# The first pair's first half taken one head at a time, with its row maxima brought to the scores by one copy

## The chip, the cores and the metric

One core of a Trainium2 chip runs the whole program. The metric is device time in microseconds (us) of one execution, as the median of several runs. PE is TensorE (PEld its weight loads), DVE VectorE, ACT ScalarE, POOL GpSimd, SP the engine whose queue issues most transfers.

## The reference, cut to what matters

Attention with a mask from clusters (a query sees the keys whose nearest of 16 centroids is its own), then two dense layers.

```python
# q, k, v: (2, 8, 768, 64); x: 1536 tokens of 512; w_in: 512 x 2048, w_out: 2048 x 512
mask = q_assign[:, :, :, None] == k_assign[:, :, None, :]
scores = scale * np.matmul(q, k.transpose(0, 1, 3, 2))
scores = np.where(mask, scores, -1000000000.0)
scores = scores - np.max(scores, axis=-1, keepdims=True)
attn = np.exp(scores)
attn = attn / (np.sum(attn, axis=-1, keepdims=True) + 1e-09)
x = np.matmul(attn, v)            # then, with heads joined:
h = np.maximum(x @ w_in, 0.0);  x = h * h @ w_out
h = x @ w_in2;  g = h * np.cos(h);  out = g @ w_out2
```

## The kernel before

**Tiling.** The 16 heads go in 8 pairs. In a pair's tiles one head (j = 0) lies in partitions 0 to 63 and the other (j = 1) in 64 to 127, so a matmul for one head contracts over 64 partitions, one half of the PE array's rows. The 768 tokens are two halves of 384, or six tiles of 128. Each of q and k is split into a rounded part (`hq`, `hk`) and a rest (`lq`, `lk`); they lie in tiles that the profile calls `set`. `ext` holds `xq` and `xk`, one-hot rows of the clusters, which make the mask.

**A half of a pair**, in steps, each a small function:

- `s_max` (matmul L579): four matmuls fill one *unit*, a piece of PSUM of two banks, [128 queries, 2, 384]: for each head the product of one query tile with one half of the keys, and the mask's product on top. There are three units, shared by nearly all steps here. `s_largest` (L589) takes the largest over the keys on DVE and so gives the unit back. Six of these (three query tiles, two halves of keys) give the maxima of both heads over 384 queries.
- `max_parts` (L598, DVE) joins the two halves of the keys, `max_cast` (L604, ACT) spreads each maximum over 32 columns, `max_rows` (L613, PE) turns them into rows by three matmuls with the identity, `max_keep` (L620, ACT) copies those out of PSUM, `stage_max` (L627, two transfers) puts them into the outer rows of `lq`.
- `scores` (L648): eight matmuls, four products for each of the two heads, give a unit [128 keys, 2 heads, 384 queries]; the fourth product reads `lq` with the maxima and so subtracts them. Of the first three units of all (`APART`) the fourth product stands apart, in `scores_end`. `exponent` (L662, ACT) reads the unit and gives it back, `add_up` (L674, POOL) adds the exponentials, `pv` (L682, PE) multiplies by v into `o_ps`, `sums` (L699), `move_out` (L737) and others finish the half.

In all matmuls of `s_max` and `scores` the two heads alternate: j = 0, j = 1, j = 0, and so on.

**The masks of the following pairs** are made in between, from `sims` (L466) over `by_token` (L484), `at_max` (L507), `compare` (L514) and `one_hot` (L520) to `keep_one_hot` (L527). `keep_warm` (L774) are matmuls without a use, which stand on PE where it would wait.

**Order.** `PLACES` gives every step a number, by hand; all steps are sorted by it and written out once, and each engine runs its own instructions in that order. The dense layers (L885, L939) come after, also in a fixed order.

Of the kernel before, what the change touches and what calls it, by code (L numbers as in the profile page):

```python
# [9 lines left out]
F32 = mybir.dt.float32  # L10
# [6 lines left out]
AX = mybir.AxisListType.X  # L17
# [12 lines left out]
N_WARM = 23  # L30
# [8 lines left out]
        3, 2, 24, 58, 60, 79, 176, 179, 301, 332, 418, 529, 597, 613, 733, 701,  # L39
    ),  # L40
    "low_part": (
        9, 42, 70, 59, 69, 126, 295, 217, 351, 404, 472, 531, 641, 630, 787, 715,
    ),
    "load_raw": (
        25, 240, 0, 43, 283, 140, 178, 428, 239, 287, 480, 350, 417, 634, 481, 580, 828, 583, 644, 898,
    ),
    "sims": (
        6, 28, 77, 227, 338, 504, 581, 696,
    ),
    "keep_sims": (  # L50
        12, 35, 78, 228, 341, 505, 582, 697,
    ),
    "by_token": (
        21, 47, 96, 252, 376, 523, 653, 724,
    ),
    "largest": (
        22, 48, 117, 259, 407, 524, 654, 726,
    ),
    "spread": (
        23, 75, 118, 272, 425, 546, 661, 734,  # L60
    ),
    "at_max": (
        31, 80, 132, 275, 433, 547, 663, 755,
    ),
    "compare": (
        33, 83, 151, 289, 437, 548, 675, 779,
    ),
    "stage_own": (
        87, 196, 251, 397, 352, 611, 616, 819,
    ),  # L70
    "stage": (
        10, 5, 111, 88, 222, 226, 331, 303, 443, 416, 555, 571, 649, 673, 809, 795,
    ),
    "one_hot_k": (
        40,
    ),
    "one_hot_q": (
        44,
    ),
    "keep_k": (  # L80
        41,
    ),
    "keep_q": (
        45,
    ),
    "max_parts": (
        82, 128, 173, 223, 305, 356, 406, 464, 545, 578, 664, 707, 781, 823, 887, 941,
    ),
    "max_cast": (
        89, 131, 174, 235, 313, 364, 427, 466, 554, 579, 665, 728, 782, 824, 888, 942,  # L90
    ),
    "max_rows": (
        90, 136, 194, 253, 321, 377, 435, 491, 564, 608, 666, 729, 783, 836, 903, 951,
    ),
    "max_keep": (
        91, 139, 195, 255, 322, 378, 436, 492, 566, 609, 667, 730, 786, 839, 904, 959,
    ),
    "stage_max": (
        98, 141, 210, 256, 347, 379, 444, 500, 584, 612, 668, 744, 802, 862, 913, 960,
    ),  # L100
    "one_hot": (
        93, 191, 318, 442, 562, 680, 780,
    ),
    "keep_one_hot": (
        95, 192, 319, 449, 563, 686, 791,
    ),
    "stage_oh": (
        120, 224, 345, 450, 599, 689, 817,
    ),
    "squares": (  # L110
        7, 26,
    ),
    "norms": (
        8, 27,
    ),
    "inverses": (
        11, 34,
    ),
    "keep_warm": (
        13, 14, 15, 16, 17, 18, 19, 20, 29, 30, 36, 37, 38, 39, 46, 49, 50, 51, 52, 53, 64, 65, 66,  # L120
    ),
    "constants_own": (
        1, 32, 4,
    ),
    "constants": (
        81, 94,
    ),
    "move_out": (
        202, 231, 320, 380, 446, 509, 569, 656, 693, 745, 838, 865, 899, 948, 981,
    ),  # L130
    "sums": (
        242, 360, 493, 606, 714, 834, 949, 996,
    ),
    "move_sums": (
        243, 361, 494, 610, 717, 841, 956, 997,
    ),
    "deal_sums": (
        244, 363, 501, 615, 718, 842, 958, 1001,
    ),
    "invert": (  # L140
        276, 385, 508, 643, 727, 847, 968, 1011,
    ),
    "store_inverse": (
        277, 392, 510, 658, 756, 870, 969,
    ),
    "load_inverse": (
        286, 398, 514, 672, 765, 900, 974,
    ),
    "divide": (
        326, 339, 429, 457, 561, 592, 725, 721, 804, 769, 930, 931, 1005, 1000,  # L150
    ),
    "combine_high": (
        327, 342, 465, 458, 575, 607, 731, 732, 844, 784, 950, 935, 1006, 1002,
    ),
    "combine_low": (
        329, 368, 537, 476, 589, 671, 797, 762, 849, 902, 980, 986, 1010, 1007,
    ),
    "s_max": (
# [5 lines left out]
    ),  # L164
    "s_largest": (
# [5 lines left out]
    ),  # L171
    "scores": (
# [15 lines left out]
    ),  # L188
    "add_up": (
# [5 lines left out]
    ),  # L195
# [22 lines left out]
def tile_kernel(ctx: ExitStack, tc: tile.TileContext, lead, behind, q, k, v, directions, centroids, w1i, w1o, w2i, w2o, out):  # L218
    nc = tc.nc
# [373 lines left out]
    def max_parts(n, hf):
# [3 lines left out]
        m1 = ap.tile([P, 2 * HT], F32, tag="m1", name=f"m1{n}{hf}", bufs=2)  # L597
# [25 lines left out]
    def stage_max(n, hf, e=nc.sync):  # L623
# [622 lines left out]
```

## Time and profile before

| | us |
|---|---|
| median of 3 runs | 747.66 (747.25 to 747.78) |
| the profiled execution | 747.83 |
| its span in the trace | 746.1 |

The profiled execution is 0.17 above the median, and 1.7 of it lies outside the span. On the page and in the views, busy time is the union of an engine's records; the records of matmuls overlap, so a stretch in which PE is busy throughout can still hold small waits. PE is busy in 737.4 of 746.1 us, DVE in 577.4, ACT in 352.9, POOL in 248.3.

### The profile page before, as it was taken

Reading aid. Unit: us, or ns where it says so; the run is one execution under the profiler, and the core shown is the slowest. Engines: PE = TensorE matmul, PEld = TensorE weight load, DVE = VectorE, ACT = ScalarE, POOL = GpSimd, SP = SyncE. Lnnn points to the kernel's source line nnn. Section 1 sums busy time; section 2 is a strip of 40 time slices with the busy share of each in tenths; the row PEclk is TensorE's granted clock in tenths of the full one; section 3 lists DMA queues with packets and bytes.
Section 4 is the critical chain, followed back from the end, with each engine's and each line's share of the span. In section 5 each row is a group of like instructions: output and inputs, shape, how many; then the busy total and the mean of one; then the engine's idle time right before and its main releaser. Section 6 shows DMA issues by size and latency. Waiting matters only on the chain.

```text
span 746.1 us, 11041 instructions
## 1 busy us (share of the span) xinstructions
PE 737.4 (99%) x4143; PEld 573.2 (77%) x4143; DVE 577.4 (77%) x913; ACT 352.9 (47%) x595; POOL 248.3 (33%) x249
## 2 busy tenths in 40 slices
PE   8999999999999999999999999999999999999997
PEld 5766766666667888888888888888887888888886
DVE  6897988896689999697883149699998766676664
ACT  5655656564555464635445344544334333343332
POOL 8899998999996200000000000022221000000000
PEclk9999999999999999999999999999999999999999
DMA  6525433314534610474000037420001000010001
GB/s 209 165 88 160 124 119 103 113 45 142 196 116 161 225 57 1 144 245 147 29 0 1 1 95 238 147 84 1 0 2 55 2 1 1 0 57 1 0 1 56
DMA packets 40589, 62.18 MB, mean 83 GB/s; under 512 B 6228, under 2 KB 28760, under 8 KB 40536
## 3 DMA queue, kind: packets, MB, share of 16 engines
q1 hardware_dynamic: 40200, 60.65, 25.4%
q10 hardware_dynamic: 336, 0.84, 0.3%
q8 instruction: 32, 0.52, 0.3%
q14 instruction: 21, 0.17, 0.1%
HBM read 48.46 MB, written 5.29 MB: 72 GB/s over the span
## 4 chain that ended last, share of the span: by engine, by line
PE 85%; DVE 12%; issue 1%; DMA 1%; ACT 1%; SPq 0%; DVEq 0%
PE bank L939 30%; PE bank L885 15%; PE o_ps L885 14%; PE unit L648 9%; PE o_ps L682 9%; PE unit L579 5%; DVE ews L908 3%; DVE ews L907 1%; DVE m L589 1%; DVE ews L919 1%; DVE top L324 1%; PE o_ps L466 1%; DVE aux L322 1%; PE o_ps L699 1%; DVE ews L910 1%
## 5 line engine op out<-in xcount | busy, mean ns | idle before, releaser
L674 POOL TENSOR_TENSOR acc<-acc,p 128x384 f32<-128x384 f32 x128 | 142.1, 1143 | 1.0 <-ACT p L662 0.8
L939 PE MATMUL bank<-w,ewr 128*128 128x512 f32 x576 | 138.2, 389 | 0.6 <-DVE w L317 0.6
L939 PE MATMUL bank<-ewr,w 128*128 128x512 f32 x576 | 138.5, 389 | 0.0
L924 POOL TENSOR_TENSOR ewr<-ews,ewr 128x512 fp32r<-128x512 f32 x22 | 29.5, 1340 | 299.6 <-ACT ewr L920 289.2
L885 PE MATMUL bank<-xh,w 128*128 128x512 f32 x392 | 128.7, 390 | 0.0
L939 PEld LDWEIGHTS bank<-w,ewr 128*128 128x128 f32 x576 | 108.0, 188 | 23.4 <-DVE w L317 1.0
L939 PEld LDWEIGHTS bank<-ewr,w 128*128 128x128 f32 x576 | 108.0, 188 | 22.7 <-ACT ews L901 0.3
L885 PE MATMUL o_ps<-xh,w 128*128 128x512 f32 x376 | 123.3, 389 | 0.0
L589 DVE TENSOR_REDUCE m<-unit 128x2 f32<-128x768 f32 x96 | 88.9, 950 | 25.7 <-PE unit L579 22.6
L662 ACT ACTIVATE p<-unit 128x768 f32<-128x768 f32 x96 | 73.4, 813 | 50.8 <-PE unit L648 44.7
L924 DVE TENSOR_TENSOR ewr<-ews,ewr 128x512 fp32r<-128x512 f32 x74 | 51.7, 698 | 51.6 <-ACT ewr L903 46.9
L885 PEld LDWEIGHTS bank<-xh,w 128*128 128x128 f32 x392 | 73.5, 188 | 16.5 <-issue 1.2
L911 ACT ACTIVATE ews<-ews,narrow_t 128x512 f32<-128x512 f32 x48 | 34.8, 725 | 100.5 <-DVE ews L910 100.5
L885 PEld LDWEIGHTS o_ps<-xh,w 128*128 128x128 f32 x376 | 70.5, 188 | 14.5
L885 PE MATMUL bank<-xl,w 128*128 128x512 f32 x196 | 76.3, 389 | 0.0
L885 PE MATMUL o_ps<-xl,w 128*128 128x512 f32 x188 | 73.1, 389 | 0.0
L682 PE MATMUL o_ps<-p,rawv 128*64 128x384 f32 x384 | 68.1, 493 | 0.0
L648 PE MATMUL unit<-set,set 64*128 64x384 f32 x512 | 67.1, 342 | 0.1
L905 DVE TENSOR_SCALAR ews<-ews 128x512 f32<-128x512 f32 x48 | 20.3, 422 | 43.4 <-ACT ews L915 43.1
L324 DVE SCALAR_TENSOR_TENSOR top<-wraw,top 128x512 uint32<-128x512 uint32 x64 | 51.1, 799 | 1.6
L648 PEld LDWEIGHTS unit<-set,set 64*128 64x128 f32 x512 | 45.3, 184 | 6.8 <-ACT p L662 2.6
L322 DVE SCALAR_TENSOR_TENSOR aux<-wraw,aux 128x512 f32<-128x512 uint32 x64 | 49.1, 767 | 1.6
(141 smaller groups left out, 1026.4 us busy)
## 6 DMA issues: line engine op xcount, KB each, us to landing
wraw<-in_moe_w_in_dram SPq DMA_DIRECT2D x32, 512.0 KB, 3.9
wraw<-in_moe_w_out_dram SPq DMA_DIRECT2D x32, 512.0 KB, 4.3
ext<-set SPq DMA_DIRECT2D x32, 96.0 KB, 2.9
rawv<-in_v_dram SPq DMA_DIRECT2D x8, 384.0 KB, 3.5
rb<-row SPq DMA_DIRECT2D x14, 192.0 KB, 3.5
fq<-in_q_dram SPq DMA_DIRECT2D x6, 384.0 KB, 4.1
fk<-in_k_dram SPq DMA_DIRECT2D x6, 384.0 KB, 3.7
held<-kept SPq DMA_DIRECT2D x8, 256.0 KB, 3.1
```

The lines of the kernel that those rows point to most:

```text
L322: cost(690, lambda: ve.scalar_tensor_tensor(restf, low, 2.0**-32, rest, ALU.mult, ALU.add)),
L324: cost(690, lambda: ve.scalar_tensor_tensor(top, high, 0xC0000000, top, ALU.bitwise_and, ALU.bitwise_or)),
L579: nc.tensor.matmul(u[:, j, :HALF], lhsT=a[r, qs], rhs=b[r, ks], start=(p == 0), stop=(p == 1))
L589: nc.vector.tensor_reduce(d["m"][:, i, :, kh], u[:, :, :HALF], AX, ALU.max)
L648: nc.tensor.matmul(u[:, j, :HALF], lhsT=a[r], rhs=b[r, qs], start=(p == 0), stop=(p == len(ops) - 1))
L662: nc.scalar.activation(t, u[:, :, :HALF], AF.Exp, scale=SCALE)
L674: nc.gpsimd.tensor_tensor(accs[hb][:, j], a[:, j], ptiles[u_][:, j], ALU.add)
L682: nc.tensor.matmul(o_ps[0][j * D : (j + 1) * D, :HALF], lhsT=raw[n, "v"][:, kt, j, :], rhs=t[:, j], start=(kt == 0), stop=(kt == NT - 1),)
L885: nc.tensor.matmul(ph, lhsT=w[:, a, :], rhs=x[blk][:, a, :], start=(a == i == 0), stop=(a == KD - 1 and i == 2))
L911: nc.scalar.activation(e2, e2, AF.Sin, bias=hpi)
L924: e.tensor_tensor(al, e2, ah.bitcast(F32), ALU.subtract)
L939: nc.tensor.matmul(y, lhsT=a, rhs=b, start=(idx in opens and i == 0), stop=(idx in closes and i == 2))
```

## The change

For the first half of the first pair alone (units 0 to 5), a unit holds one head: its two banks are the two halves of the keys in `s_max`, and two tiles of keys in `scores`. One reduction over both banks (`AXY`) then gives the final maximum of a head, into a small tile `by_head`; three units finish a head. `max_rows` for this half takes a column of `by_head`, repeated 128 times, as its weights, three matmuls for each head, so that every row of the result holds the maxima; `max_keep` copies the 32 rows that `lq` needs straight into it. `max_parts`, `max_cast` and `stage_max` fall away for this half. `add_up` and `pv` of this half take their operands by the new split. Three `keep_warm` go (`N_WARM` 23 to 20), and the numbers in `PLACES` are new up to about 400, above that nearly all are the old ones less 4.

```diff
-N_WARM = 23
+N_WARM = 20
...
     "s_max": (
-        61, 62, 54, 67, 71, 73, 86, 84, 97, 100, 103, 116, 163, 171, 154, 148, 125, 149, 200, 218, 197, 214,
+        58, 60, 66, 68, 50, 74, 82, 80, 86, 94, 100, 119, 156, 169, 146, 137, 126, 132, 195, 208, 207, 188,
...
     "scores": (
-        102, 119, 106, 123, 112, 146, 161, 165, 159, 167, 157, 175, 233, 215, 229, 260, 247, 249, 284, 292,
...
+        101, 96, 116, 107, 121, 138, 149, 159, 154, 163, 151, 165, 227, 222, 218, 257, 244, 241, 267, 277, 272,
...
+    by_head = prepp.tile([P, 64], F32R, name="by_head")[:, :NT].rearrange("p (j t) -> p j t", j=2)
+
     def s_max(u_):
         n, c = divmod(u_, SP)
         i, kh = divmod(c, 2)
         d = pd[n]
         u = unit()
-        qs, ks = slice(i * P, (i + 1) * P), slice(kh * HALF, (kh + 1) * HALF)
+        if u_ < NT:
+            kh, i = divmod(u_, HT)
         for p, (a, b) in enumerate(((d["hq"], d["hk"]), (xq[n % 2], xk[n % 2]))):
             for j in range(2):
-                r = slice(j * D, (j + 1) * D)
+                head, part = (kh, j) if u_ < NT else (j, kh)
+                r = slice(head * D, (head + 1) * D)
+                qs, ks = slice(i * P, (i + 1) * P), slice(part * HALF, (part + 1) * HALF)
                 nc.tensor.matmul(u[:, j, :HALF], lhsT=a[r, qs], rhs=b[r, ks], start=(p == 0), stop=(p == 1))
...
-        nc.vector.tensor_reduce(d["m"][:, i, :, kh], u[:, :, :HALF], AX, ALU.max)
+        if u_ < NT:
+            nc.vector.tensor_reduce(by_head[:, u_ // HT, u_ % HT : u_ % HT + 1], u[:, :, :HALF], AXY, ALU.max)
+        else:
+            nc.vector.tensor_reduce(d["m"][:, i, :, kh], u[:, :, :HALF], AX, ALU.max)
...
-    def max_rows(n, hf):
+    def max_rows(n, hf, j=None):
         d = pd[n]
         u = unit()
+        if j is not None:
+            for t in range(HT):
+                nc.tensor.matmul(
+                    u[:, 0, t * P : (t + 1) * P], lhsT=by_head[:, j, t : t + 1].to_broadcast([P, P]), rhs=identr,
+                    start=True, stop=True,
+                )
+            d["mru", j] = u
+            return
...
-    def max_keep(n, hf):
-        d = pd[n]
+    def max_keep(n, hf, j=None):
+        d = pd[n]
+        if j is not None:
+            u = d.pop(("mru", j))
+            nc.scalar.copy(d["lq"][OUTER[j], hf * HALF : (hf + 1) * HALF], u[OUTER[j], 0, :HALF])
+            give(u)
+            return
...
         for p in mine:
-            a, b = ops[p]
             for j in range(2):
-                r = slice(j * D, (j + 1) * D)
+                head, t = (j, kt) if u_ >= NT else (kt // HT, kt % HT * 2 + j)
+                ks = slice(t * P, (t + 1) * P)
+                ops = (
+                    (d["hk"][:, ks], d["hq"]), (d["lk"][:, ks], d["hq"]), (xk[i][:, ks], xq[i]),
+                    (block(sets[n % 3], t), d["lq"]),
+                )
+                a, b = ops[p]
+                r = slice(head * D, (head + 1) * D)
...
+        if hb == 0:
+            for i in (0, 1) if kt == 1 else (kt,):
+                j = i // HT
+                y, t = accs[hb][:, j], ptiles[i]
+                a, b = (t[:, 0], t[:, 1]) if i % HT == 0 else (y, t[:, 0])
+                nc.gpsimd.tensor_tensor(y, a, b, ALU.add)
+                if i % HT:
+                    nc.gpsimd.tensor_tensor(y, y, t[:, 1], ALU.add)
+            return
...
         for j in range(2):
+            i, c = (u_, j) if u_ >= NT else (kt // 2 + j * HT, kt % 2)
...
-                o_ps[0][j * D : (j + 1) * D, :HALF], lhsT=raw[n, "v"][:, kt, j, :], rhs=t[:, j],
+                o_ps[0][j * D : (j + 1) * D, :HALF], lhsT=raw[n, "v"][:, kt, j, :], rhs=ptiles[i][:, c],
```

The lines of the kernel move by 5 to 35; L579 becomes L584, L589 L596 (this half) and L598, L613 L622 (this half) and L630, L620 L637 (this half) and L642, L648 L674, L682 L717.

**On PE, from the seventh `s_max` to the first unit of `scores`.** `set0_0`, `set0_1` are the first pair's `hq`, `hk`; `set0_2`, `set0_3` its `lq`, `lk`; `x2` counts matmuls. Before:

```order
L579 MATMUL unit1_71<-set0_1_101,set0_0_100 128x384 x2
L579 MATMUL unit1_71<-ext0_1_113,ext0_0_112 128x384 x2
L579 MATMUL unit2_72<-set0_1_101,set0_0_100 128x384 x2
L579 MATMUL unit2_72<-ext0_1_113,ext0_0_112 128x384 x2
L613 MATMUL unit0_70<-identr_78,set0_3_103 64x128 x3
...
L484 MATMUL o_ps1_66<-ident_73,sc2_333 128x128 x3
L579 MATMUL unit0_70<-set0_1_101,set0_0_100 128x384 x2
...
L579 MATMUL unit2_72<-set0_1_101,set0_0_100 128x384 x2
...
L648 MATMUL unit1_71<-set0_0_100,set0_1_101 128x384 x2
```

Now, from `sims` of the third pair on:

```order
L466 MATMUL o_ps1_66<-fk2_289,cb_120 32x384 x2
L622 MATMUL unit2_72<-identr_78,by_head_119 128x128 x3
L584 MATMUL unit0_70<-set0_1_101,set0_0_100 128x384 x2
...
L584 MATMUL unit2_72<-set0_1_101,set0_0_100 128x384 x2
...
L622 MATMUL unit1_71<-identr_78,by_head_119 128x128 x3
L584 MATMUL unit0_70<-set0_1_101,set0_0_100 128x384 x2
...
L484 MATMUL o_ps1_66<-ident_73,sc2_340 128x128 x3
...
L584 MATMUL unit1_71<-set0_1_101,set0_0_100 128x384 x2
L584 MATMUL unit1_71<-ext0_1_113,ext0_0_112 128x384 x2
L674 MATMUL unit0_70<-set0_0_100,set0_1_101 128x384 x2
```

Two groups of `max_rows` stand where one stood, one for each head, and the first `scores` still follow the tenth `s_max`. The rows name no partitions: in the first six `s_max` and `scores` both matmuls of an `x2` are now of one head.

**On ACT, around the first exponentials.** `mxb`, `sc` are of the masks of later pairs. Before:

```order
L440 CAST set2_1_109<-fk2_271 128x768
L604 CAST set0_3_103<-m100_341 128x192
L620 CAST mr00_362<-unit0_70 64x384
L627 DMA set0_2_102<-mr00_362 32x384
L662 ACTIVATE p0_403<-unit1_71 128x768
```

Now:

```order
L440 CAST set2_1_109<-fk2_289 128x768
L637 CAST set0_2_102<-unit2_72 32x384
L476 ACTIVATE sc2_340<-o_ps1_66,narrow_t_85 128x384
L637 CAST set0_2_102<-unit1_71 32x384
L688 ACTIVATE p1_384<-unit0_70 128x768
```

A cast, a copy and a transfer (with its twin on SP) became two copies; the first exponential is that of the second unit.

## Rows read from the trace of the kernel before

**Rows 1.** The page, parts 1 and 2: busy us, share, instructions; granted clock.

```profile
PE 737.4 (99%) x4143; PEld 573.2 (77%) x4143; DVE 577.4 (77%) x913; ACT 352.9 (47%) x595; POOL 248.3 (33%) x249
...
PEclk9999999999999999999999999999999999999999
```

**Rows 2.** Busy time by stretch: PE, PEld, DVE, ACT, POOL, clock, DMA.

```profile
13.20:25.00 11.80, 10.50 (x83) 6.39 (x85) 11.58 (x17) 5.00 (x9) 11.33 (x9) 1.00 0.49 145
25.00:60.00 35.00, 35.00 (x307) 23.87 (x309) 30.98 (x44) 20.17 (x33) 30.32 (x27) 1.00 0.44 132
60.00:230.00 170.00, 169.83 (x1413) 113.52 (x1410) 141.25 (x164) 100.46 (x173) 164.61 (x155) 1.00 0.43 133
```

**Rows 3.** The chain that ended last, 11 to 32 us: start, us, what.

```profile
13.94 5.29 DVE m L589 x6
...
19.25 0.17 DVE m L598
...
22.11 1.83 DVE m L589 x2
...
23.99 1.84 PE unit L648 x16
```

**Rows 4.** Timeline of ACT: start, us, engine, line, idle before.

```profile
19.71 0.35 ACT L604 CAST set<-m 128x192 fp32r<-128x192 f32 x1
20.55 0.47 ACT L620 CAST mr<-unit 64x384 fp32r<-64x384 f32 x1 [0.48 <-PE unit L613]
```

**Rows 5.** Timeline of PE, same columns, from 24.8 us: units one behind the other.

```profile
24.85 0.62 PE L648 MATMUL unit<-set,set 64*128 64x384 f32 x4
25.31 0.34 PE L648 MATMUL unit<-ext,ext 64*128 64x384 f32 x2
25.49 0.34 PE L648 MATMUL unit<-set,set 64*128 64x384 f32 x2
25.67 0.33 PE L579 MATMUL unit<-set,set 64*128 64x384 f32 x2
```

**Rows 6.** The weight loads (PEld) of the same stretch.

```profile
25.32 0.19 PEld L648 LDWEIGHTS unit<-set,set 64*128 64x128 f32 x2
```

**Rows 7.** A stretch of the dense layers, PE alone: matmuls of 512 columns.

```profile
300.00:350.00 50.00, 50.00 (x222) 1.00 0.55 179
```

**Rows 8.** Timeline of DVE from 13.2 us.

```profile
13.94 5.28 DVE L589 TENSOR_REDUCE m<-unit 128x2 f32<-128x768 f32 x6 [0.15 <-PE unit L579]
...
19.34 0.55 DVE L514 TENSOR_TENSOR free_xh<-free_xl,unit 128x384 bf16<-128x384 f32 x1
19.80 1.81 DVE L589 TENSOR_REDUCE m<-unit 128x2 f32<-128x768 f32 x2
21.53 0.67 DVE L527 TENSOR_SCALAR free_xl<-unit,oh_above,oh_scale 128x384 fp32r<-128x384 f32 x1
```

**Rows 9.** Timeline of PE at the first scores.

```profile
22.25 0.62 PE L648 MATMUL unit<-set,set 64*128 64x384 f32 x4
...
23.12 0.45 PE L579 MATMUL unit<-set,set 64*128 64x384 f32 x2
23.41 0.34 PE L579 MATMUL unit<-ext,ext 64*128 64x384 f32 x2
23.59 1.02 PE L648 MATMUL unit<-set,set 64*128 64x384 f32 x6
...
24.62 0.34 PE L648 MATMUL unit<-set 64*128 64x384 f32 x2
```

**Rows 10.** Timeline of PE around the end of the first half.

```profile
38.58 2.16 PE L682 MATMUL o_ps<-p,rawv 128*64 128x384 f32 x12
40.67 0.34 PE L520 MATMUL o_ps<-eq,first_of 128*128 128x384 bf16 x1
```

**Rows 11.** Timeline of PE from 13.2 us: `sims` and `at_max` among the maxima.

```profile
17.23 0.52 PE L466 MATMUL o_ps<-fq,cb 128*32 128x384 f32 x2
...
18.34 0.55 PE L507 MATMUL unit<-ident,free_xl 128*128 128x128 f32 x3
```

More of the change, by code (lines that the diff above doesn't have):

```diff
@@ L16 @@
 ALU = mybir.AluOpType
-AX = mybir.AxisListType.X
+AX, AXY = mybir.AxisListType.X, mybir.AxisListType.XY
 PSUM = bass.MemoryType.PSUM
@@ L46 @@
     ),
     "sims": (
-        6, 28, 77, 227, 338, 504, 581, 696,
+        7, 21, 75, 209, 319, 500, 577, 692,
     ),
     "keep_sims": (
-        12, 35, 78, 228, 341, 505, 582, 697,
+        9, 40, 78, 210, 332, 501, 578, 693,
     ),
     "by_token": (
-        21, 47, 96, 252, 376, 523, 653, 724,
+        18, 42, 91, 251, 372, 519, 649, 720,
     ),
     "largest": (
-        22, 48, 117, 259, 407, 524, 654, 726,
+        19, 51, 99, 254, 403, 520, 650, 722,
     ),
     "spread": (
-        23, 75, 118, 272, 425, 546, 661, 734,
+        22, 56, 105, 284, 421, 542, 657, 730,
@@ L61 @@
     ),
     "at_max": (
-        31, 80, 132, 275, 433, 547, 663, 755,
+        25, 64, 129, 286, 429, 543, 659, 751,
     ),
     "compare": (
-        33, 83, 151, 289, 437, 548, 675, 779,
+        28, 65, 157, 287, 433, 544, 671, 775,
     ),
     "stage_own": (
-        87, 196, 251, 397, 352, 611, 616, 819,
+        69, 153, 292, 393, 352, 607, 612, 815,
     ),
     "stage": (
-        10, 5, 111, 88, 222, 226, 331, 303, 443, 416, 555, 571, 649, 673, 809, 795,
+        27, 8, 113, 104, 221, 216, 347, 310, 439, 412, 551, 567, 645, 669, 805, 791,
@@ L73 @@
     ),
     "one_hot_k": (
-        40,
+        33,
     ),
     "one_hot_q": (
-        44,
-    ),
-    "keep_k": (
-        41,
-    ),
-    "keep_q": (
-        45,
+        36,
+    ),
+    "keep_k": (
+        43,
+    ),
+    "keep_q": (
+        44,
+    ),
+    "max_rows": (
+        76, 85, 131, 184, 255, 303, 373, 431, 487, 560, 604, 662, 725, 779, 832, 899, 947,
+    ),
+    "max_keep": (
+        77, 87, 135, 185, 256, 304, 374, 432, 488, 562, 605, 663, 726, 782, 835, 900, 955,
     ),
@@ L86 @@
     "max_parts": (
-        82, 128, 173, 223, 305, 356, 406, 464, 545, 578, 664, 707, 781, 823, 887, 941,
+        122, 171, 228, 276, 329, 402, 460, 541, 574, 660, 703, 777, 819, 883, 937,
     ),
     "max_cast": (
[L90 to L96, printed above, removed]
+        128, 172, 232, 300, 359, 423, 462, 550, 575, 661, 724, 778, 820, 884, 938,
@@ L97 @@
     ),
     "stage_max": (
-        98, 141, 210, 256, 347, 379, 444, 500, 584, 612, 668, 744, 802, 862, 913, 960,
+        136, 217, 264, 320, 375, 440, 496, 580, 608, 664, 740, 798, 858, 909, 956,
     ),
     "one_hot": (
-        93, 191, 318, 442, 562, 680, 780,
+        92, 183, 301, 438, 558, 676, 776,
     ),
     "keep_one_hot": (
-        95, 192, 319, 449, 563, 686, 791,
+        93, 187, 302, 445, 559, 682, 787,
     ),
     "stage_oh": (
-        120, 224, 345, 450, 599, 689, 817,
+        125, 220, 349, 446, 595, 685, 813,
@@ L109 @@
     ),
     "squares": (
-        7, 26,
+        3, 20,
     ),
     "norms": (
-        8, 27,
+        4, 37,
     ),
     "inverses": (
-        11, 34,
+        5, 39,
     ),
     "keep_warm": (
-        13, 14, 15, 16, 17, 18, 19, 20, 29, 30, 36, 37, 38, 39, 46, 49, 50, 51, 52, 53, 64, 65, 66,
+        10, 11, 12, 13, 14, 15, 16, 17, 23, 24, 29, 30, 31, 32, 41, 45, 46, 47, 48, 49,
     ),
     "constants_own": (
-        1, 32, 4,
+        0, 38, 2,
     ),
     "constants": (
-        81, 94,
+        63, 83,
@@ L127 @@
     ),
     "move_out": (
-        202, 231, 320, 380, 446, 509, 569, 656, 693, 745, 838, 865, 899, 948, 981,
+        186, 230, 307, 376, 442, 505, 565, 652, 689, 741, 834, 861, 895, 944, 977,
     ),
     "sums": (
-        242, 360, 493, 606, 714, 834, 949, 996,
+        237, 355, 489, 602, 710, 830, 945, 992,
     ),
     "move_sums": (
-        243, 361, 494, 610, 717, 841, 956, 997,
+        238, 356, 490, 606, 713, 837, 952, 993,
     ),
     "deal_sums": (
-        244, 363, 501, 615, 718, 842, 958, 1001,
+        252, 357, 497, 611, 714, 838, 954, 997,
@@ L139 @@
     ),
     "invert": (
-        276, 385, 508, 643, 727, 847, 968, 1011,
+        253, 381, 504, 639, 723, 843, 964, 1007,
     ),
     "store_inverse": (
-        277, 392, 510, 658, 756, 870, 969,
+        296, 388, 506, 654, 752, 866, 965,
     ),
     "load_inverse": (
-        286, 398, 514, 672, 765, 900, 974,
+        298, 394, 510, 668, 761, 896, 970,
     ),
     "divide": (
-        326, 339, 429, 457, 561, 592, 725, 721, 804, 769, 930, 931, 1005, 1000,
+        308, 317, 425, 453, 557, 588, 721, 717, 800, 765, 926, 927, 1001, 996,
@@ L209 @@
-        961, 970, 972, 993, 995, 998, 999,
+        34, 103, 110, 111, 115, 134, 148, 161, 162, 179, 180, 181, 214, 215, 243, 250, 271, 285, 295, 366, 378,
+        392, 401, 430, 466, 471, 509, 549, 592, 594, 627, 646, 688, 702, 712, 762, 882, 886, 925, 933, 939,
+        957, 966, 968, 989, 991, 994, 995,
     ),
     "begin_moe": (
-        858,
+        854,
     ),
@@ L587, in s_largest @@
         if "m" not in d:
-            d["m"] = ap.tile([P, NT, 2, 2], F32, tag="m", name=f"m{n}", bufs=2)
-        nc.vector.tensor_reduce(d["m"][:, i, :, kh], u[:, :, :HALF], AX, ALU.max)
+            m = ap.tile([P, R], F32, tag="m", name=f"m{n}", bufs=2)[:, : 4 * NT]
+            d["m"] = m.rearrange("p (t j h) -> p t j h", j=2, h=2)
+        if u_ < NT:
+            nc.vector.tensor_reduce(by_head[:, u_ // HT, u_ % HT : u_ % HT + 1], u[:, :, :HALF], AXY, ALU.max)
+        else:
+            nc.vector.tensor_reduce(d["m"][:, i, :, kh], u[:, :, :HALF], AX, ALU.max)
         give(u)
@@ L596, in max_parts @@
         mm = d["mm"] = sets[n % 3][3][:, S : S + HT * 2 * R].rearrange("p (t r) -> p t r", t=HT)
-        m1 = ap.tile([P, 2 * HT], F32, tag="m1", name=f"m1{n}{hf}", bufs=2)
+        m1 = ap.tile([P, R], F32, tag="m1", name=f"m1{n}{hf}", bufs=2)[:, : 2 * HT]
         nc.vector.tensor_reduce(m1.rearrange("p (t j) -> p t j", j=2), m, AX, ALU.max)
@@ L621, in max_keep, with stage_max @@
         give(u)
-    def stage_max(n, hf, e=nc.sync):
+    def stage_max(n, hf):
         d = pd[n]
@@ L626, in stage_max @@
         for j in range(2):
-            (e if j else nc.sync).dma_start(
+            nc.sync.dma_start(
                 d["lq"][OUTER[j], hf * HALF : (hf + 1) * HALF].bitcast(F32), mr[j * R : (j + 1) * R].bitcast(F32)
@@ L678, in pv @@
         hf, kt = divmod(c, NT)
-        t = ptiles[u_]
-        assert u_ not in unread
         for j in range(2):
+            i, c = (u_, j) if u_ >= NT else (kt // 2 + j * HT, kt % 2)
+            assert i not in unread
             nc.tensor.matmul(
-                o_ps[0][j * D : (j + 1) * D, :HALF], lhsT=raw[n, "v"][:, kt, j, :], rhs=t[:, j],
+                o_ps[0][j * D : (j + 1) * D, :HALF], lhsT=raw[n, "v"][:, kt, j, :], rhs=ptiles[i][:, c],
                 start=(kt == 0), stop=(kt == NT - 1),
@@ L1126, in tile_kernel @@
         for hf in range(2):
-            for f in maxima:
-                at(f, n, hf, *((nc.scalar,) if f == stage_max and n == hf == 0 else ()))
+            for f in maxima if n or hf else ():
+                at(f, n, hf)
+            for f in () if n or hf else maxima[2:4]:
+                for j in range(2):
+                    at(f, n, hf, j)
     for i in range(2):
@@ L1154, in tile_kernel @@
             at(add_up, u_)
-            at(pv, u_)
+        for w in range(2 * u_ - NT, 2 * u_ - NT + 2) if u_ < NT else range(u_, min(u_ + 1, NU - 3)):
+            if w >= 0:
+                at(pv, w)
     for i in range(n_early + n_late):
```

20 lines of the change are left out of this document (8 added, 12 removed), and 56 rows, old and new, of the table PLACES.

## The prediction

> **What bounds the kernel now.** The page first: PE is busy in 99% of the span at the full granted clock, every other engine in 77% or less [rows 1]. By stretch, PE has no idle time from 25 to 60 us and 0.17 us in the next 170, while POOL (164.61 of 170) and DVE come behind it [rows 2]. Work that is added to PE's row there moves the end by as much, unless it fills waits that the overlapping records hide. The one stretch near the change where PE does idle is 13.2 to 25 us: 10.50 of 11.80, with DVE at 11.58 [rows 2]. There DVE paces: its reductions of one unit follow each other.
>
> So the question is who ends the waits in that stretch. The chain of waits [rows 3] answers: it runs through the reductions of L589, the small joining reduction of L598, again L589, and then straight to PE's `scores`. It does not pass the cast or copy on ACT [rows 4], nor a transfer: when the maxima's rows landed, PE was still waiting for DVE to give a unit back. What the change takes away (0.35 us of cast on ACT, two transfers, 0.17 us on DVE [rows 3, 4]) is therefore hardly on the path that sets the end. What it adds to PE must be priced exactly.
>
> **How PE works on a unit today.** A unit of `scores` begins at 24.85 us and its last two matmuls at 25.49; the next unit begins at 25.67 [rows 5]. From 25.31 on, two matmuls begin every 0.175 us. They are of 384 columns each. The price of one such stream alone is seen in the dense layers: 222 recorded matmuls of 512 columns in 50.00 us, 0.225 each [rows 7], which for 384 columns is 0.169 us. So the two matmuls of a pair, one in either half of the array's rows (64 of 128), stream side by side in the time of one. A unit of `s_max` (four matmuls) costs PE 0.35, one of `scores` (eight) 0.70, and some 0.11 more where PE restarts after a wait: 23.12 to 23.41 for a first pair, against 0.175 [rows 9].
>
> **What the change does to that.** In units 0 to 5 both matmuls of each pair belong to one head, so both want the same 64 rows. No row here shows two such matmuls in succession. Bounds from the nearest rows: if they still went side by side, nothing is added; if they queue, each takes a turn of its own, 0.175 us by the pairs, where each half already takes one matmul per 0.175 us [rows 5], or 0.169 by the dense layers [rows 7]. I take 0.175: it is what one half of the rows does today, its weight load (0.19 us) beginning just behind the start of the matmul before it, 25.32 against 25.31 [rows 5, 6]. The Trainium skill says the same of what no row shows: "TensorEngine Tiling (Array Packing)", Key Properties, lets different tiles run in parallel, and these would be one tile. Then `s_max` of units 0 to 5 takes 0.70 and not 0.35 each, +2.1 in all, and `scores` 1.40 and not 0.70, +4.2 in all. Where a unit of one head follows one of the other without a wait, the last matmul of the one and the first of the next still meet.
>
> **Up to the first scores: +1.0.** The order on PE puts the first `scores` behind the tenth `s_max`, as before, and they need the unit that the reduction of the ninth gives back. I walk DVE.
> - Before: six reductions from 13.94 in 5.28 us, hence (5.28 - 0.95)/5 = 0.87 from one to the next with 0.95 for the last; the joining one; `compare` 19.34 to 19.80, 0.46; two more; `keep_one_hot` ends at 22.20, and PE's first `scores` start at 22.25 [rows 8, 9].
> - After: the first unit is full 0.35 later, 14.29. Three reductions to 16.90, `compare` to 17.36, three more to 19.97. A reduction over both banks reads the same 768 elements per partition, and I leave it at 0.95.
> - Meanwhile PE, behind `compare` (which gives `at_max`'s unit back at about 17.9), does the sixth `s_max` (0.11 + 0.70), then `sims` (1.1 us between its first row and the next step's [rows 11], of which some wait for a load), then the first `max_rows`, then the seventh `s_max`, ready at about 20.4. DVE waits some 0.4 us.
> - Three reductions from 20.4 end at 20.4 + 2 x 0.87 + 0.95 = 23.1, and the first `scores` start at about 23.25: 1.0 later than 22.25.
>
> So of the 2.1 us on the maxima 0.35 and 0.4 show on DVE, the rest hides under its pace. DVE makes that good for now, since the joining reduction goes and `keep_one_hot` stands later; the ninth reduction ends where it did (22.11 + 0.95 = 23.06 [rows 3]). But before, PE's first `scores` hung on `keep_one_hot`, and now they hang on that reduction. The two groups of `max_rows`, the two copies on ACT and the smaller number of `keep_warm` lie in this stretch under DVE and cost nothing; without that cover a group of `max_rows` is about 0.4 us with the changes of tile shape.
>
> **From the first scores to the end of the first half's `pv`: +3.15.** From 22.25 to 40.67 [rows 9, 10] both kernels do the same on PE: twelve units of `scores`, nine of `s_max`, six of `pv`, one `at_max`, one `max_rows`.
> - Six units at 0.70 more: +4.2.
> - Before, PE waits here three times for a unit: 22.25 + 0.11 + 3 x 0.175 = 22.89 against 23.12; 23.59 + 0.175 = 23.76 against 23.99 (the row begins at 23.59 with the odd last pair); 24.62 + 0.175 = 24.80 against 24.85 [rows 5, 9]. That is 0.52, with three restarts of 0.11 0.85. A unit of 1.40 lets the ACT and DVE keep up, so this goes: -0.85.
> - About two or three meetings of different heads: -0.45.
> - One `pv` now stands between `scores` and `s_max` by itself, a change of tile shape more: +0.25. It is 24.62 to 24.85 less 0.175, with a restart [rows 5, 9], doubled.
>
> **Later: +0.3.** Up to about 75 us the order differs step by step (a unit waits some tenths for DVE between two `scores` of the second pair, in my walk); from there it is the old one, and a shift stays, PE being without gaps [rows 2]. Between nil and the 0.85 of the first stretch I take 0.3. POOL begins `add_up` about 1 us later and PE asks for the sums 4 us later, so that costs nothing. The queue of SP loses two small transfers; the loads of the third pair go ahead of the first weights, and its k still waits for POOL's `low_part`.
>
> Sum: 1.0 + 3.15 + 0.3 = 4.45. The profiled execution took 747.83; that gives 752.3, and against the median, 0.17 lower, **752.1**.
>
> **Rivals.**
> - *Matmuls of one half of the rows also go side by side* (the change as it may be meant). Then nothing of 6.3 is added, the first `scores` start within 0.1 of 22.25 (DVE: 13.94 + nine reductions and `compare`), and -0.85 + 0.25 remain: 747.66 - 0.5 = about 747.2, not slower. For it: nothing in a row; against it, pairs need 0.175, the time of a whole stream. This decides: with 36 pairs, the gain is eaten as soon as a pair of one head takes over 0.175 + 0.5 / 36 = 0.19. 7%, of which a third ends over 0.2% faster, by waits in the maxima that go as well.
> - *PE has room that the records hide.* If POOL (30.32 of 35 us busy) or DVE (30.98) [rows 2] set the pace between 25 and 60 us, a part of 3.15 drowns. Half of it would give 750.5. Against it, PE is busy in 35.00 of 35.00 there [rows 2]. 9%.
> - *The weight load can't run under a matmul in its own half.* Then each matmul in a queue costs 0.285, as a first pair does [rows 9], so 0.11 x 72 = 8 more for the 72 of the six units of each kind, less what DVE hides: about 758. Rows 5 and 6 speak against it: in either half the next load begins with the matmul. 4%. By the Trainium skill, "TensorE: Matmul & The Clock Gate", Part 3, weight loads overlap matmuls in flight only in other row groups, which is this rival; its Part 2 allows a background buffer too, and with that the sum stands.
> - *A load comes late.* `sims` of the third pair needs its k before about 18.5 us; if that came 1.5 later, the start of `scores` would too: 753.6. 5%, within the range.
>
> **How the numbers follow.** The forecast has 75%, with 751.2 to 753.6 for its own errors (0.169 for 0.175 takes 0.2; no wait of DVE 0.4; nothing later 0.3; all of 0.85 later adds 0.5, a late load 1.5). To hold 8 in 10 the range goes to 749.3, between the rival of room and that of side by side, and up to 754.8, short of the weight loads. A measurement of this kernel can tell about 0.2%, 1.5 us, from no change: slower by over 0.2% is above 749.2, which the forecast and nearly all of room, weight loads and late load give: 0.88. Within: 0.07. Faster: 0.05.
>
> **What would show it.** In the changed trace: in the first six units of `s_max` and `scores` single matmuls 0.17 us apart and not pairs, 1.4 us per unit of `scores`; first `scores` at about 23.2 us; the end of the first half's `pv` (40.67 before [rows 10]) some 4 us later; no wait for ACT's copies. Pairs at 0.175 would prove the forecast wrong, and so would units of 2 us.

## The result, and the profile after

The changed kernel takes 752.26 us (median of 4 runs, 751.55 to 752.37) against 747.58 (747.25 to 747.78): ratio 1.0061, 95% interval 1.0047 to 1.0074. The predicted time was 752.1. The profiled execution took 752.26, its span is 750.5.

The page and the stretches, which answer to [rows 1, 2] (the columns are the same):

```profile
PE 740.9 (99%) x4143; PEld 578.0 (77%) x4143; DVE 575.3 (77%) x912; ACT 352.7 (47%) x595; POOL 247.7 (33%) x249
...
13.20:25.00 11.80, 11.23 (x73) 8.13 (x74) 10.83 (x15) 5.17 (x10) 11.33 (x9) 1.00 0.53 163
25.00:60.00 35.00, 34.93 (x290) 24.97 (x288) 28.12 (x40) 20.02 (x33) 25.53 (x24) 1.00 0.38 110
60.00:230.00 170.00, 168.97 (x1420) 111.74 (x1417) 138.13 (x166) 99.86 (x174) 165.01 (x155) 1.00 0.43 127
```

PE is as busy as before but does less: between 25 and 60 us 290 recorded matmuls where there were 307, and DVE, ACT and POOL do less too. From 13.2 to 25 PE is busy in 11.23 us instead of 10.50 and DVE in 10.83 instead of 11.58. DVE's timeline answers to [rows 8]:

```profile
14.22 2.69 DVE L596 TENSOR_REDUCE by_head<-unit 128x1 fp32r<-128x768 f32 x3 [0.46 <-PE unit L584]
...
17.28 2.68 DVE L596 TENSOR_REDUCE by_head<-unit 128x1 fp32r<-128x768 f32 x3
20.47 2.69 DVE L598 TENSOR_REDUCE m<-unit 128x2 f32<-128x768 f32 x3 [0.51 <-PE unit L584]
```

The first unit is full 0.28 later than in [rows 8]; DVE waits 0.51 ahead of the seventh reduction; the ninth ends at 20.47 + 2.69 = 23.16. Then PE begins the first `scores`, at 23.21, where it was 22.25 [rows 9]. PE's timeline, first ahead of the seventh `s_max` (19.81) and then from the first `scores` on:

```profile
18.55 0.52 PE L466 MATMUL o_ps<-fq,cb 128*32 128x384 f32 x2
...
19.33 0.55 PE L622 MATMUL unit<-identr,by_head 128*128 128x128 f32 x3
19.81 0.45 PE L584 MATMUL unit<-set,set 64*128 64x384 f32 x2
...
23.21 0.97 PE L674 MATMUL unit<-set,set 64*128 64x384 f32 x4
24.02 0.52 PE L674 MATMUL unit<-ext,ext 64*128 64x384 f32 x2
24.20 0.44 PE L584 MATMUL unit<-set,set 64*128 64x384 f32 x1
24.38 0.33 PE L674 MATMUL unit<-set 64*128 64x384 f32 x1
24.48 0.34 PE L584 MATMUL unit<-ext,ext 64*128 64x384 f32 x1
24.55 0.33 PE L674 MATMUL unit<-set,set 64*128 64x384 f32 x1
24.73 0.33 PE L584 MATMUL unit<-set,set 64*128 64x384 f32 x1
...
28.63 0.35 PE L584 MATMUL unit<-ext,ext 64*128 64x384 f32 x2
29.05 0.96 PE L674 MATMUL unit<-set,set 64*128 64x384 f32 x4
29.85 0.51 PE L674 MATMUL unit<-ext,ext 64*128 64x384 f32 x2
30.20 0.33 PE L674 MATMUL unit<-set 64*128 64x384 f32 x1
30.37 0.34 PE L674 MATMUL unit<-set,set 64*128 64x384 f32 x1
30.63 0.87 PE L717 MATMUL o_ps<-p,rawv 128*64 128x384 f32 x4
...
42.69 2.16 PE L717 MATMUL o_ps<-p,rawv 128*64 128x384 f32 x12
44.78 0.34 PE L520 MATMUL o_ps<-eq,first_of 128*128 128x384 bf16 x1
```

The unit that begins at 29.05 shows the price: its last matmuls begin at 29.85 (two), 30.20 and 30.37, four of one head, (30.37 - 29.85) / 3 = 0.173 us apart, which is what a pair of both heads took before [rows 5]. The first half's `pv` ends at 44.78, 4.11 later than at 40.67 [rows 10].

ACT's timeline (answering [rows 4]) has two copies instead of cast, copy and transfer:

```profile
19.96 0.47 ACT L637 CAST set<-unit 32x384 fp32r<-32x384 f32 x1 [1.48 <-DVE by_head L596]
...
21.61 0.47 ACT L637 CAST set<-unit 32x384 fp32r<-32x384 f32 x1 [0.71 <-PE unit L622]
```

The second ends at 22.08, 1.1 ahead of the first `scores`. The chain of waits (answering [rows 3]) passes the first copy, which gives back the unit that PE's eighth `s_max` takes at 20.48, but not the second, and later one exponential:

```profile
17.36 2.61 DVE by_head L596 x3
19.97 0.47 ACT set L637
...
28.19 0.81 ACT p L688
29.00 0.04 issue
29.05 1.66 PE unit L674 x8
```

The chain follows PE here, but DVE, too, works without a gap from 20.47 to 23.16, and PE begins the first `scores` only when DVE's ninth reduction is done. So the first copy delays PE, and by these rows not the first `scores`.

### The profile page after: what moved, and what is told of

Read it like the earlier page. It is cut to its first block, busy times and chain, and to the rows that moved or that the text cites. A ratio compares the mean times of both kernels' runs of the same rounds, so it can differ in the third digit from the quotient of the medians.

```text
span 750.5 us, 11028 instructions
## 1 busy us (share of the span) xinstructions
PE 740.9 (99%) x4143; PEld 578.0 (77%) x4143; DVE 575.3 (77%) x912; ACT 352.7 (47%) x595; POOL 247.7 (33%) x249
## 4 chain that ended last, share of the span: by engine, by line
PE 84%; DVE 11%; issue 1%; DMA 1%; ACT 1%; SPq 0%; DVEq 0%
PE bank L974 29%; PE bank L920 15%; PE o_ps L920 14%; PE unit L674 10%; PE o_ps L717 8%; PE unit L584 5%; DVE ews L943 3%; DVE ews L942 1%; DVE ews L954 1%; DVE top L324 1%; PE o_ps L734 1%; DVE aux L322 1%; DVE ews L945 1%; DVE ews L940 1%; DMA ext<-ot 1%
## 5 line engine op out<-in xcount | busy, mean ns | idle before, releaser
L709 POOL TENSOR_TENSOR acc<-acc,p 128x384 f32<-128x384 f32 x120 | 133.2, 1143 | 2.0 <-ACT p L688 2.0
L598 DVE TENSOR_REDUCE m<-unit 128x2 f32<-128x768 f32 x90 | 83.6, 950 | 31.2 <-PE unit L584 28.4
L674 PE MATMUL unit<-set,set 64*128 64x384 f32 x512 | 68.9, 341 | 0.1
L717 PE MATMUL o_ps<-p,rawv 128*64 128x384 f32 x384 | 68.1, 493 | 0.0
L674 PEld LDWEIGHTS unit<-set,set 64*128 64x128 f32 x512 | 47.7, 184 | 6.2 <-ACT p L688 1.9
```

The costliest lines, as they stand in the source:

```text
L674: nc.tensor.matmul(u[:, j, :HALF], lhsT=a[r], rhs=b[r, qs], start=(p == 0), stop=(p == len(ops) - 1))
L709: nc.gpsimd.tensor_tensor(accs[hb][:, j], a[:, j], ptiles[u_][:, j], ALU.add)
L717: nc.tensor.matmul(o_ps[0][j * D : (j + 1) * D, :HALF], lhsT=raw[n, "v"][:, kt, j, :], rhs=ptiles[i][:, c], start=(kt == 0), stop=(kt == N ...
```

## Experiments

Each kernel is compared with the kernel before on the same chip. Some executions of kernels whose maxima go head by head had a mean granted clock of 0.988 to 0.995 and took 1 to 6 us longer, one of them 12; where they are part of a median, the times at a clock of 1.0 stand beside it (e12 shows where the clock was low).

**e1: the changed kernel with the scores by pairs again**, the rest as changed:

```diff
-                head, t = (j, kt) if u_ >= NT else (kt // HT, kt % HT * 2 + j)
+                head, t = j, kt
```

> The changed kernel with one part taken back: the scores of the first six units hold both heads again (one key tile per unit), with the sums and the products with v by it; maxima by head, their two copies and all places stay. Theory Q (two matmuls of one half of the array's rows queue at 0.175 us each): 24 pairs no longer queue, 4.2 us of PE time less, of which up to 1 us had been won back where units of different heads meet; so 2.5 to 3.5 us under the changed kernel, 748.8 to 749.8, with 0.70 us per unit of scores in the trace. Theory P (the new places cost the time, by waits on other engines or transfers): no change, 752 to 752.5.

Measured 749.58 (748.66 to 753.18, 10 runs), ratio 1.0039 (1.0023 to 1.0055); the seven executions at a clock of 1.0 took 748.7 to 749.9, as Q said. About 3 us of the loss went. Beginnings come by pairs again, (25.52 - 25.35) = 0.17 for two:

```profile
23.45 0.61 PE L674 MATMUL unit<-set,set 64*128 64x384 f32 x4
...
25.35 0.34 PE L674 MATMUL unit<-ext,ext 64*128 64x384 f32 x2
25.52 0.52 PE L674 MATMUL unit<-set,set 64*128 64x384 f32 x4
...
42.37 0.34 PE L520 MATMUL o_ps<-eq,first_of 128*128 128x384 bf16 x1
```

The half still ends at 42.37, 1.70 after the kernel before. Of that, 1.20 lies ahead of the first `scores` (23.45 against 22.25), with the maxima. The other 0.50 lies behind them: from there to the end of `pv` it is 42.37 - 23.45 = 18.92, against 18.42 before, though the scores go by pairs again. That part belongs to the new order.

**e2: the kernel before with the scores by head alone**, maxima as before (the edits of `scores`, `add_up` and `pv`, four `pv` a little later).

> The kernel before with that part alone: the scores of the first six units each hold one head and two key tiles; maxima, transfers and places as before, but for the first two products with v, which stand a little later since they need the fourth unit. Theory Q: 4.2 us more on PE, less the three waits of 0.85 us in all that a unit of 1.4 us fills and up to 0.8 us where heads meet: 2.5 to 3.4 us over the kernel before, 750.1 to 751.0. Theory P: within 0.5 us of the kernel before.

Measured 750.43 (750.05 to 750.75, 4 runs), ratio 1.0042 (1.0026 to 1.0059), as Q said. The half ends at 43.83, 3.16 later:

```profile
22.93 0.96 PE L652 MATMUL unit<-set,set 64*128 64x384 f32 x4
...
43.83 0.34 PE L520 MATMUL o_ps<-eq,first_of 128*128 128x384 bf16 x1
```

But in this execution the first `scores` already begin 0.68 late, at 22.93, behind steps that the edit leaves as they were. From there it is 43.83 - 22.93 = 20.90, which is 2.48 over the 18.42 before. The same part seen from the other side, the changed kernel against e1, is 21.57 - 18.92 = 2.65. So one head at a time in the scores costs about 2.5 to 2.65 us.

**e3 and e11: the kernel before with the maxima by head alone**, at the old places.

```diff
+        if u_ < NT:
+            nc.vector.tensor_reduce(by_head[:, u_ // HT, u_ % HT : u_ % HT + 1], u[:, :, :HALF], AXY, ALU.max)
...
-            for f in maxima:
+            for f in maxima if n or hf else ():
...
+            for f in () if n or hf else maxima[2:4]:
+                for j in range(2):
+                    at(f, n, hf, j)
```

> The kernel before with the other part alone: the maxima of the first half by head, two groups of three matmuls and two copies in place of the joining reduction, the cast, the copy and the transfers; scores by pairs, places as before. Theory Q: the first unit is full 0.35 us later and DVE waits some tenths more behind the sixth unit, so the first scores start 0.5 to 1.2 us later: 748.1 to 748.8, with four single matmuls per unit 0.17 us apart. Rival (the shorter way of the maxima pays on the path): at or under 747.2.

> The kernel of e3 once more, for the clock: three of its five executions had a mean granted clock of 0.993 to 0.995. By theory H some do here as well, and a trace of one shows the lower clock in the stretch of the maxima, before 25 us; by the rival (a disturbance of that chip) all are at 1.0, 749.5 to 750.3.

e3 took 750.82 (5 runs, 749.78 to 762.09; ratio 1.0043, 1.0029 to 1.0057, without the 762.09), at a clock of 1.0 749.78 and 749.94; e11 749.74 (748.43 to 751.39, 6 runs; 1.0031, 1.0020 to 1.0043). Slower by more than the 0.6 to 1.3 us expected, and e3's rival is out: the shorter way of the maxima gains nothing. The half ends at 41.91 and 41.78, 1.1 to 1.2 later, and the first `scores` begin at 23.47 and 23.38. What comes on top of that lies later and differs between the two (spans 748.2 and 746.7); that part wasn't settled. One of e11's six executions (751.39) had a clock of 0.995, so the low clock isn't of one chip alone; its trace is of another execution, so it shows no stretch for H.

**e4: the kernel before, where from the second half on the four matmuls of one head stand ahead of the four of the other** in each of 90 units:

```diff
-        for p in mine:
...
-            for j in range(2):
...
+        pairs_ = [(p, j) for p in mine for j in range(2)]
+        if u_ >= NT:
+            pairs_ = [(p, j) for j in range(2) for p in mine]
+        for p, j in pairs_:
```

> The kernel before, with the eight matmuls of each unit of scores from the second half of the first pair on (90 units) written four of one head first and four of the other behind; nothing else changes. It asks how far matmuls of the other half of the rows may start ahead of earlier ones. If all start in the order written, a unit takes some 1.05 us in place of 0.70: 0.35 x 90 = 31 us, about 779. If PE starts a matmul of the free half ahead of queued ones of the busy half, as the changed kernel's trace shows at 24.20 us, little is lost: 747.5 to 751.

Measured 749.89 (749.20 to 750.50, 5 runs), ratio 1.0035 (1.0022 to 1.0048): 2.5 us, not 31. From one whole unit to the next:

```profile
60.70 0.43 PE L650 MATMUL unit<-ext,ext 64*128 64x384 f32 x2
60.88 0.44 PE L650 MATMUL unit<-set 64*128 64x384 f32 x2
...
61.40 0.45 PE L650 MATMUL unit<-ext,ext 64*128 64x384 f32 x2
61.57 0.45 PE L650 MATMUL unit<-set,set 64*128 64x384 f32 x2
```

61.40 - 60.70 = 0.70, the time of a unit by pairs, though the program has the heads one after the other: PE begins matmuls of the idle half of its rows ahead of earlier ones that wait for the busy half.

**e5 and e12: the changed kernel with the heads in turn**, units 0, 3, 1, 4, 2, 5 in the six places of the scores:

```diff
     "scores": (
-        101, 96, 116, 107, 121, 138, 149,
+        96, 107, 121, 101, 116, 138, 149,
```

> The changed kernel with the six one-head units of the first half's scores dealt anew to the same six places, so that the heads alternate from unit to unit (units 0, 3, 1, 4, 2, 5 in the order in which PE meets them, where the changed kernel has 1, 0, 3, 2, 4, 5); nothing else is moved but the closing products and exponentials that belong to them. Theory O (PE starts matmuls of the free half of its rows ahead of queued ones of the busy half, so that most of the 4.2 us of queueing can be won back where neighbours are of different heads): the end of the first half's pv comes 1 to 2.5 us earlier than in the changed kernel (44.78), and the time is 749.8 to 751.3. Rival T (only the last matmul of one unit and the first of the next meet, 0.175 us for each of two or three more changes of head): 751.8 to 752.2.

> The kernel of e5 once more, since three of its six executions had a mean granted clock of 0.991 and its median says little. By the executions at a clock of 1.0 it should take 750.1 to 751.5, 0.5 to 1.5 us under the changed kernel (theory O in size halved); by the rival T, 751.8 or more. If executions at the lower clock come again, at 755 to 756, a trace of one would show in which stretch the clock was low.

e5: 753.41 (750.07 to 755.78, 6 runs), ratio 1.0077 (1.0053 to 1.0101), with three executions at a clock of 0.991; the three at 1.0 took 750.07, 751.15 and 751.47. e12: 753.46 (750.22 to 756.19), 1.0076 (1.0049 to 1.0103); the three at 1.0 took 750.22, 750.92 and 750.93. The six have a median of 750.9, about 1 under the changed kernel. e5's half ends at 44.14, 0.64 earlier: O in kind, but under its 1 to 2.5. Its first and its last unit still stand alone on PE:

```profile
23.27 0.97 PE L674 MATMUL unit<-set,set 64*128 64x384 f32 x4
24.08 0.52 PE L674 MATMUL unit<-ext,ext 64*128 64x384 f32 x2
...
28.34 0.34 PE L584 MATMUL unit<-ext,ext 64*128 64x384 f32 x1
28.43 0.97 PE L674 MATMUL unit<-set,set 64*128 64x384 f32 x4
29.24 0.52 PE L674 MATMUL unit<-ext,ext 64*128 64x384 f32 x2
```

One of e12's executions at the lower clock was the profiled one. Its page and its stretches (columns as in [rows 2], the granted clock third from the end):

```profile
PEclk9699999999999999999999999999999999999999
...
13.00:18.00 5.00, 4.32 (x25) 3.54 (x26) 4.51 (x7) 3.47 (x6) 4.82 (x5) 1.00 0.41 124
18.00:18.50 0.50, 0.50 (x4) 0.27 (x2) 0.50 (x2) 0.39 (x1) 0.50 (x1) 0.81 0.89 211
18.50:19.00 0.50, 0.50 (x5) 0.20 (x8) 0.50 (x2) 0.00 (x0) 0.50 (x1) 0.50 0.97 328
...
31.50:32.00 0.50, 0.50 (x5) 0.50 (x5) 0.47 (x2) 0.50 (x1) 0.00 (x0) 0.54 0.84 234
32.00:32.50 0.50, 0.50 (x9) 0.50 (x7) 0.50 (x1) 0.28 (x1) 0.00 (x0) 1.00 0.99 328
```

From about 18.3 to 32.0 us the clock is 0.50, that is 1.2 and not 2.4 GHz. The half ends at 49.14, 5.0 after e5's, and the span is 754.4 against 749.7.

**e6: the kernel before with the direct rows alone**: maxima by pairs and joined as before, but into `by_head`; two groups of `max_rows` and two copies; no cast, no transfer.

```diff
+        if n == hf == 0:
+            nc.vector.tensor_reduce(by_head.rearrange("p j t -> p t j"), m, AX, ALU.max)
+            return
```

> The kernel before with one part of the change alone: the maxima are made in pairs of heads as before and joined by the same small reduction on DVE, but it writes them into the small tile, max_rows takes a repeated column of that for each head, and max_keep copies straight into the rows that the scores read; the cast and the two transfers of the first half are gone. Theory N (the cast and the transfers lay under DVE's reductions, so removing them gains nothing; a second group of three matmuls and a second copy lie there too): within 0.6 us of the kernel before, 747.0 to 748.2. Rival G (the shorter way pays, and the head-by-head order is what hides it): 746.6 or less.

Measured 748.44 (747.82 to 749.11, 11 runs), ratio 1.0014 (1.0005 to 1.0022). No gain, as N said, but a loss of 0.9, above N's upper end. A row of PE's timeline in the kernel before, and then the rows of e6:

```profile
20.80 0.32 PE L520 MATMUL unit<-free_xh,first_of 128*128 128x384 bf16 x1 [0.29 <-DVE m L589]
```

```profile
20.06 0.55 PE L618 MATMUL unit<-identr,by_head 128*128 128x128 f32 x3
20.83 0.55 PE L618 MATMUL unit<-identr,by_head 128*128 128x128 f32 x3 [0.23 <-DVE m L591]
...
22.75 0.51 PE L666 MATMUL unit<-set,set 64*128 64x384 f32 x4
```

The second group needs a second of the three units and waits 0.23 for DVE to give it back. That wait is not new: before, PE waited 0.29 at the same place, ahead of L520. New is the group behind it, after which L520 begins at 21.22 and no longer at 20.80. The first `scores` begin 0.50 later than at 22.25 [rows 9].

**e7: the changed kernel with one group of transfers earlier** (`stage_oh` of the fourth pair, place 349 to 346.5).

> The changed kernel with one step moved: the transfers that put the fourth pair's one-hot rows in place (L563) are issued ahead of the load of a later q and of the high rows' transfers (L456), by which they stood in the changed kernel's queue on SP at 73.2 to 75.2 us. Theory L (the wait of 0.99 us at 80.0 us, PE for these rows, is a new loss of the changed order that is partly made up later anyway): the wait is gone, and the time is 0.2 to 0.8 us under the changed kernel, 751.4 to 752.0. Rival: the loss is made up wholly, or another transfer comes late in its place: within 0.2 us of the changed kernel.

In the changed kernel this wait is new; the timelines of SP's queue and of PE show its cause, transfers that stand behind a load of 384 KB:

```profile
74.50 0.58 SPq L427 DMA_DIRECT2D fq<-in_q_dram  x1
75.19 2.42 SPq L563 DMA_DIRECT2D ext<-ot  x4
...
81.00 0.53 PE L584 MATMUL unit<-ext,ext 64*128 64x384 f32 x2 [0.99 <-DMA ext<-ot]
```

e7: 753.98 (750.81 to 757.83, 6 runs), ratio 1.0090 (1.0060 to 1.0120), with three executions at 0.988 to 0.991; the three at 1.0 took 750.81, 751.42 and 751.72. The wait is down to 0.17, on other transfers (`ext<-set`). By these three some tenths are won, as L said; the traces don't show it, since the span is that of e8's (750.0), where the wait was 0.6. (In e9's trace, of the same order, it is 1.43: the wait differs from one execution to the next.)

**e8: the changed kernel once more, and e9: with three `keep_warm` back** between its third and fourth unit of the maxima.

> The changed kernel itself once more, beside the other three on one chip, as their measure: 751.9 to 752.5 by every theory.

> The changed kernel with the three keep_warm that it dropped put back, where PE waits for DVE between the third and the fourth unit of the maxima. In earlier runs the kernels whose maxima go head by head (the changed one, e1, e3, e5, e7) had executions with a mean granted clock of 0.988 to 0.995, 4 to 6 us longer than their others, and the kernels whose maxima go by pairs (before, e2, e4, e6) had none. Theory W (PE does too little before the first scores, and the dropped keep_warm are missed): all executions at a clock of 1.0 and 751.6 to 752.4. Theory H (it is the one-head order of the maxima itself, since e3 has all 23 keep_warm and shows it too): some executions of this kernel still have the lower clock, at 755 to 758, the others 751.6 to 752.4.

e8: 752.07 (ratio 1.0073, 1.0051 to 1.0095), five executions from 751.64 to 752.35 and one of 757.73 at 0.988. e9: 752.08 (751.46 to 752.68, 5 runs), ratio 1.0063 (1.0049 to 1.0076), all at 1.0: the three cost nothing where they stand. By itself this says nothing on W and H, since e10, without them, ran on the same chip at 1.0 throughout too. But e3 and e11 have all 23 `keep_warm`, and four of their eleven executions ran at a lower clock, which speaks against W.

**e10: the edits of e5 and e7 together.**

> The changed kernel with the edits of e5 and of e7 together: heads in turn in the first half's scores, and the fourth pair's one-hot rows ahead of the next load. Theory: the two lie in different places (25 to 45 us and 80 us) and add up, about 0.7 and 0.4 us, so that executions at a clock of 1.0 take 750.3 to 751.3; it stays slower than the kernel before. Rival: the wait at 80 us absorbs what is won earlier, and the sum is no better than the better of the two, 751.2 or more.

Measured 750.24 (749.90 to 750.78, 5 runs), ratio 1.0040 (1.0027 to 1.0052). They add up, 1.8 under e8 and e9, and come out just under the range expected: the end of the span is 0.8 earlier than e5's (748.9 against 749.7), whose wait at 80 us was 0.8. No version of the change beats the kernel before.

## Why the prediction was right, step by step

- **The mechanism.** Two matmuls of one head queue at 0.174 us (0.175 taken); a unit of scores takes 8 x 0.174 = 1.39. Side by side is out (e1, e2). The weight load hides in its own half too: 0.174 from start to start has no room for 0.285. That rival, from the Trainium skill's "TensorE: Matmul & The Clock Gate", Part 3, does not hold here.
- **Up to the first scores, +1.0.** 23.21 - 22.25 = 0.96. The walk along DVE held row by row: 14.22 (14.29), a wait of 0.51 (0.4), the ninth reduction at 23.16 (23.1). That nothing would be paid for the copies was right by the rows: the first one delays PE, but under DVE's reductions. That the two groups of `max_rows` cost nothing holds for the second alone, and e6 shows that even this is so only in the changed order of places; in the old one it costs 0.5. The first group stands on PE's way to the seventh `s_max` and takes 0.48 there (19.33 to 19.81), for which the walk put no time. It met its 20.4 all the same (20.47), by luck: `sims`, put at 1.1, took 0.78 (18.55 to 19.33), and the sixth `s_max` began at 17.76 and not at 17.9.
- **First scores to the end of `pv`, +3.15.** Measured (44.78 - 23.21) - (40.67 - 22.25) = 21.57 - 18.42 = 3.15. That the sum is exact is luck. e1 and e2 split it in two: one head at a time in the scores costs 2.65 in the new order and 2.48 in the old one, where the terms give 4.2 - 0.85 - 0.45 = 2.90; the new order costs 0.50 with the scores by pairs, where the prediction has 0.25. Two of the terms were off within the first of these parts, too. *Meetings of heads*, -0.45: from 23.21 to 28.81 (28.63 + 0.175) PE did four units of scores and two of `s_max`; one behind the other that is 36 turns (32, and 4 for the pairs of `s_max`), 36 x 0.174 + 0.11 = 6.37, and it took 5.60, so -0.77. *Waits that go*, -0.85: a new one came, 28.81 to 29.05 for a unit that ACT gives back (its exponential ends at 29.00 in the chain of waits), with a restart 0.35. The prediction had "a unit of 1.40 lets the ACT and DVE keep up"; at this place ACT doesn't, because units that overlap become full close together. -0.77 + 0.35 = -0.42 against -0.45. The waits that went (-0.85) and the change of tile shape (+0.25) weren't measured singly; taken as predicted, with 6 x 0.69 = 4.15 the terms give 4.15 - 0.85 + 0.25 - 0.42 = 3.13.
- **Later, +0.3.** The span grew by 4.4, the half's end by 4.11, so 0.3. But this term is smaller than what executions of one kernel differ by: from the half's end to the end of the span the kernel before takes 705.4, the changed kernel 705.7 in its first trace and 705.1 in e8's. So its size isn't shown, and that it agrees is luck. A loss that the prediction did not have lies in this part: PE waits 0.99 us at 80 us (0.56 in e8) for transfers whose place in SP's queue the change moved, and e10, without it, is 0.8 shorter in span than e5. The prediction looked at that queue only for the third pair's loads, and had the 0.3 from waits for DVE. (That queue lost one small transfer, not two; the other stood on ACT's.)
- **Room on PE, a late load.** PE is busy in 34.93 of 35.00 us from 25 to 60, so nothing drowned; `sims` of the third pair didn't wait for its load.
- **The range** held. Its bounds for the last term (nothing, or all of 0.85) are about as wide as what executions differ by.

## What to carry to other kernels

Where two heads fill two halves of the PE array, see first what splitting the pair costs: here it doubled PE's time for these matmuls, only neighbours of the other head gave a part back, and the shorter way of the maxima gained nothing against it. Before removing a cast or a transfer, see whether the chain of waits passes it, and count the buffers that the shorter way takes: here, at the old places, a second group of matmuls with a PSUM unit of its own cost 0.5 us at the first `scores`, and the cast and the transfers that went gave nothing back. After new places, read each transfer that stands behind another load in its queue again.

## What the runs showed of the hardware

- **PE overtakes across the halves of its rows.** In the changed kernel the eleventh `s_max` (number 100 in `PLACES`), which stands behind a unit of scores (number 96) in PE's order, begins its matmul for the other half at 24.20 and 24.48, before that unit's last ones at 24.38 and 24.55; its own matmul for the busy half comes at 24.73. e4 gives the size: 90 units written one half after the other cost 2.5 us, where in strict order they would cost 31 by the estimate of e4. Far from all of the queueing comes back: e5 won 0.6 more of the 4.2, its first and last units having nothing of the other head beside them.
- **The clock can fall though PE is busy.** In e12's profiled execution PE was busy in 4.32 us from 13 to 18, with no gap over 0.65, when the clock went to 1.2 GHz at 18.3 and stayed there till 32.0; its span is 4.7 us longer than that of e5's trace, the same kernel at the full clock. Idle time doesn't tell such kernels from the others: from 13.2 to 25 us the kernel before has PE busy less than the changed one (10.50 against 11.23 of 11.80 us [rows 2]), and its clock never fell. What PE did before was the maxima of this half, mostly single matmuls of one half of its rows, one behind another. Of 59 executions of kernels with these maxima by head 17 had a mean clock of 0.988 to 0.995; of 73 with the maxima by pairs (before, e2, e4, e6), none. That the fall comes with the one-head order of the maxima is shown by that count. How the one leads to the other isn't, and only e12's fall was seen in a trace. Which executions it falls on, and why e9 and e10 had none in 10, stays open. The changed kernel had one in ten; its median does not hold that loss.
